# Token sums of a linear-attention layer made from one VectorE-summed tile per chunk instead of four, and the last output tile in smaller pieces

## The chip, the cores and the metric

The kernel runs on one core of a Trainium2 chip. The metric is device time in microseconds (us) of one execution, as the median of several. Engines are written as in the profile: PE is TensorE (PEld its weight loads), DVE is VectorE, ACT is ScalarE, POOL is GpSimd, SP is SyncE, which issues most transfers. L523 is line 523 of a kernel; the same instruction has a line a few numbers off in another kernel.

## The reference, cut to what matters

The input has 2048 tokens of 512 features, 32 heads of 16, and two passes of attention and feed-forward.

```python
def _A_ref(x, wqkv, wo):                   # x: 1 x 2048 x 512, H = 32, Dh = 16
    ...                                    # q, k, v from x @ wqkv
    phi = lambda t: jnp.where(t > 0, t + 1, jnp.exp(t)) + 1e-6
    pq, pk = phi(q), phi(k)
    kv = jnp.einsum("bhsd,bhse->bhde", pk, v)
    z = jnp.einsum("bhsd->bhd", pk)        # the token sum: what the change is about
    num = jnp.einsum("bhqd,bhde->bhqe", pq, kv)
    den = jnp.einsum("bhqd,bhd->bhq", pq, z)[..., None] + 1e-6
    ...                                    # (num / den) @ wo
x = x + _A_ref(_layernorm(x), A_wqkv, A_wo)
x = x + _B_ref(_layernorm(x), B_w1, B_w2)  # relu(x @ w1) @ w2, 1376 hidden
x = x + _A_ref(_layernorm(x), A_wqkv, A_wo)
x = x + _B_ref(_layernorm(x), B_w1, B_w2)
```

`z` is a sum over all tokens. Tokens lie on the 128 partitions, so somebody must add across partitions, and on this kernel that is TensorE, with a column of ones as the moving operand.

## The kernel before

The tokens are 16 tiles of 128; four tiles are a chunk. A tile of pk is 128 partitions by 512 columns of bf16. For each tile and each block of 128 columns there is one matmul with the pk block as weights and one column of ones as the moving operand; all 16 x 4 of them accumulate into four columns of one PSUM bank, from which `Zc` (the head sums) is made.

```python
def pk_unit(i):                 # the four tiles of a chunk are NCH units apart
    return (i % 4) * NCH + (i // 4)
...
def a_z_acc(lo, hi, zb, first):
    def src(i, j):
        ...                     # a GpSimd path that is switched off here
        u = pk_unit(i)
        return big[:, u * 512 + 128 * j:u * 512 + 128 * j + 128]
    def mk():
        return [(psv[:, zb, j:j + 1], src(i, j), ones[:, 0:1], first and i == lo and j == 0, i == NT - 1, True)
                for i in range(lo, hi) for j in range(4)]
    mm_group(mk, ...)           # 4 tiles x 4 blocks = 16 matmuls a chunk
```

The last output tile is finished in two halves of 256 columns, each with its last products, its own VectorE operation and its own store:

```python
prod("f3", raw(0, l1), E2, ("w2t", "b12-22"), c1, R, False)
if tail:
    rem(c1, l1, R, i1)
    out_half(i1, 1, c1)
prod("f4", summed(3), B21S, ("w2t", "b21-11"), c1, L, False)
if tail:
    rem(c1, l1, L, i1)
    out_half(i1, 0, c1)
```

All operations are recorded first and then replayed in the order of a long table, `ORDER`, found by a search; `BANKS` gives each PSUM tile its bank. An operation that two engines can do carries a letter in the table that says which does it.

## Time and profile before

| | before |
|---|---|
| time, median | 270.57 us (270.08 to 270.76, 3 runs) |
| span of the profiled execution | 268.3 us |
| PE busy | 262.3 us, 98% |
| DVE busy | 238.4 us, 89% |
| ACT busy | 199.2 us, 74% |
| one-column matmuls | 128, 25 to 26 ns from start to start |
| PE waits by name after the first 9 us | none of 0.2 us or more |

The table is read from top to bottom as one argument: PE is busy nearly always, it has no wait worth naming after the head, so PE work that goes away shortens the kernel, and anything that makes PE wait lengthens it.

### The profile page before, as it was taken

The page shows a single profiled execution, that of the slowest core. Times are in us where ns is not written, and L with a number is a line of the kernel's source. Part 1 is how long each engine was busy: PE and PEld are TensorE (multiplying, and loading weights), DVE is VectorE, ACT ScalarE, POOL GpSimd, SP SyncE. Part 2 cuts the span into 40 slices and gives each one's busy share as a digit, 9 for nine tenths or more (in the row PEclk, how much of TensorE's full clock was granted, in tenths as well). Part 3 has the DMA queues.
Part 4 walks back from the last instruction along what each step waited for, and adds up shares of the span by engine and source line. Part 5 has one row for each costly group of instructions (what it writes and reads, how often), then busy time and mean ns, then how long its engine had stood idle before and what let it go on. Part 6 is the DMA issues. An engine that isn't in the chain of part 4 may idle for free.

```text
span 268.3 us, 5363 instructions
## 1 busy us (share of the span) xinstructions
PE 262.3 (98%) x1976; PEld 172.3 (64%) x1997; DVE 238.4 (89%) x650; ACT 199.2 (74%) x434; POOL 18.7 (7%) x30
## 2 busy tenths in 40 slices
PE   7999999999999999999999999999999999999995
PEld 2444454447556878778776664455457688888884
DVE  4999986999989999998999984799889989999884
ACT  3889955999978769688867987889996878725420
POOL 4021000000110002210011000000100100200000
PEclk9999999999999999999999999999999999999999
DMA  6955882245243024402204400224363232202004
GB/s 202 381 121 82 216 286 94 101 67 119 91 123 75 0 42 86 55 0 44 56 2 78 78 5 2 98 81 85 74 157 100 41 76 45 95 2 84 16 1 156
DMA packets 47482, 23.61 MB, mean 88 GB/s; under 512 B 36736, under 2 KB 46048, under 8 KB 47456
## 3 DMA queue, kind: packets, MB, share of 16 engines
q1 hardware_dynamic: 47312, 23.21, 34.1%
q8 instruction: 15, 0.25, 0.4%
q14 instruction: 11, 0.09, 0.1%
q10 hardware_dynamic: 144, 0.07, 0.1%
HBM read 11.21 MB, written 3.15 MB: 53 GB/s over the span
## 4 chain that ended last, share of the span: by engine, by line
PE 95%; DVE 2%; DMA 1%; issue 1%; ACT 0%
PE ps L540 95%; DMA xin<-in_A_x_dram 1%; DVE bst L447 1%; DVE xn L580 0%; DVE xn L1178 0%; PE ps L503 0%; DVE mv L448 0%; DVE Tb L511 0%; DVE xn L1138 0%; ACT lnv L1169 0%; ACT rstd L1171 0%
## 5 line engine op out<-in xcount | busy, mean ns | idle before, releaser
L547 ACT ACTIVATE sqscr<-xres 128x512 bf16<-128x512 f32 x48 | 30.4, 634 | 10.8 <-DVE xres L584 5.9
L522 ACT ACTIVATE escr<-ps 128x512 bf16<-128x512 f32 x52 | 30.7, 609 | 6.8 <-PE ps L540 6.4
L520 ACT ACTIVATE big<-ps 128x512 bf16<-128x512 f32 x52 | 30.9, 613 | 1.4 <-PE ps L540 1.3
L540 PE MATMUL ps<-big,xn 128*128 128x512 bf16 x121 | 29.4, 379 | 0.4
L540 PE MATMUL ps<-gw,big 128*128 128x512 bf16 x121 | 28.9, 379 | 0.4
L1027 ACT ACTIVATE big<-ps 128x512 bf16<-128x512 f32 (+1 forms) x44 | 22.9, 533 | 6.5 <-PE ps L540 5.7
L540 PE MATMUL ps<-Tb,wqkv 128*128 128x512 bf16 x112 | 27.0, 379 | 0.0
L540 PE MATMUL ps<-wqkv,Tb 128*128 128x512 bf16 x91 | 22.7, 379 | 0.7 <-ACT Tb L510 0.3
L526 DVE TENSOR_TENSOR big<-big,escr 128x512 bf16<-128x512 bf16 x52 | 21.2, 421 | 1.5 <-ACT big L520 0.8
L540 PE MATMUL ps<-w2s,big 128*128 128x256 f16 x160 | 22.1, 272 | 0.0
L540 PEld LDWEIGHTS ps<-big,xn 128*128 128x128 bf16 x128 | 12.1, 98 | 13.9 <-issue 0.7
L540 PE MATMUL ps<-w,big 128*128 128x256 f16 (+2 forms) x113 | 20.9, 302 | 0.0
L540 PEld LDWEIGHTS ps<-gw,big 128*128 128x128 bf16 x128 | 12.2, 98 | 13.4 <-issue 0.5
L1010 ACT ACTIVATE ps<-ps 128x512 f32<-128x512 f32 (+1 forms) x29 | 15.0, 518 | 6.5 <-DVE big L1048 2.6
L540 PE MATMUL ps<-w,xin 128*128 128x256 bf16 (+1 forms) x140 | 19.5, 273 | 0.0
L540 PE MATMUL ps<-xn,xin 128*128 128x256 f16 x128 | 19.4, 273 | 0.0
L540 PE MATMUL ps<-Tb,w 128*128 128x512 bf16 x80 | 18.8, 379 | 0.0
L540 PEld LDWEIGHTS ps<-Tb,wqkv 128*128 128x128 bf16 x112 | 10.6, 98 | 12.0 <-ACT escr L522 0.3
L524 DVE TENSOR_SCALAR escr<-escr 128x512 bf16<-128x512 bf16 x52 | 14.4, 286 | 4.3 <-ACT escr L522 4.2
L540 PE MATMUL ps<-xn,w 128*128 128x256 f16 x120 | 18.2, 273 | 0.0
L540 PE MATMUL ps<-Tb,wper 128*128 128x256 bf16 x120 | 18.2, 273 | 0.0
L540 PEld LDWEIGHTS ps<-w2s,big 128*128 128x128 bf16 x160 | 15.5, 98 | 4.0 <-DVE xres L1105 0.4
(166 smaller groups left out, 548.6 us busy)
## 6 DMA issues: line engine op xcount, KB each, us to landing
xn<-rdram SPq DMA_DIRECT2D x32, 128.0 KB
wqkv<-in_A_wqkv_dram SPq DMA_DIRECT2D x3, 512.0 KB, 7.3
xin<-in_A_x_dram SPq DMA_DIRECT2D x3, 512.0 KB, 8.1
out_dram<-xn SPq DMA_DIRECT2D x3, 512.0 KB, 2.8
w<-in_B_w_dram SPq DMA_DIRECT2D x1, 1376.0 KB, 6.6
w<-in_B_w_dram SPq DMA_DIRECT2D x1, 1280.0 KB, 9.8
rdram<-rsp SPq DMA_DIRECT2D x8, 128.0 KB, 1.7
wo<-in_A_wo_dram SPq DMA_DIRECT2D x1, 512.0 KB, 10.6
```

The source lines that it names most:

```text
L447: g.add(DVE, lambda e: e.bn_stats(bst[:, i, :], xin[:, i, :]), [("xin", i)] + list(behind), [("bst", i)], C_DVE_BNST, name="bnst%d" % i)
L520: g.add(ACT, lambda e: e.activation(dst_ap, psv[:, b, :], ACTF.Identity, bias=1.0 + 1e-6, scale=1.0), [("ps", b)], [dst_key], C_ACT_PSUM, ...
L522: g.add(ACT, lambda e: e.activation(escr[:, s, :], psv[:, b, :], ACTF.Exp), [("ps", b)], [("escr", s)], C_ACT_EXP, name=name + "_exp")
L524: g.add(DVE, lambda e: e.tensor_scalar(escr[:, s, :], escr[:, s, :], 1.0, 1e-6, ALU.min, ALU.add), [("escr", s)], [("escr", s)], C_DVE_BF4 ...
L526: g.add(DVE, lambda e: e.tensor_tensor(dst_ap, dst_ap, escr[:, s, :], ALU.max), [dst_key, ("escr", s)], [dst_key], 340.0, name=name + "_phi")
L540: last = e.matmul(o, l, r, start=st, stop=sp, skip_group_check=skip)
L547: g.add(ACT, lambda e: e.activation(sqscr[:, q, :], xres[:, i, :], ACTF.Square, accum_out=dst[:, i:i + 1]), [("xres", i)], [("sqscr", q), ...
L1010: g.add_flex([(ACT, lambda e: e.activation(dst(), psv[:, src, 0:W], ACTF.Identity), cost(C_ACT_PSUM)), (DVE, lambda e: e.tensor_copy(dst() ...
L1027: g.add_flex([(ACT, lambda e: e.activation(out_ap(r, m), pv(b), ACTF.Relu), cost(C_ACT_PSUM)), (DVE, lambda e: e.tensor_scalar(out_ap(r, m ...
```

## The change

The intent is to take about two thirds of the small matmuls (84 of 128) off the engine that bounds the kernel. In seven of the eight chunks VectorE adds the four pk tiles first (two tiles plus two tiles, then the halves), into fp16, and TensorE makes the token sum of the one tile that results: 4 matmuls in place of 16. The chunk left out is the last of the first attention layer. The left half of the last output tile is cut in two quarters. `ORDER` and `BANKS` were searched anew, so instructions all over the kernel stand elsewhere.

```diff
-        def a_z_acc(lo, hi, zb, first):
-            ...
+        def a_z_acc(t, zb):
+            tiles = range(4 * t, 4 * t + 4)
+            us = [pk_unit(i) for i in tiles]
+            keys = [("big", u) for u in us] + sub_keys(us)
+            src = [unit_ap(u) for u in us]
+            if t in ZSUM[cur_layer[0] // 2]:          # ZSUM=[(0, 1, 2), (0, 1, 2, 3)]
+                zs = rhi[:].bitcast(F16)
+                hv = big[:].rearrange("p (c t k) -> p c t k", t=NCH, k=512)
+                ks = [("rhi", 0), ("rhi", 1)]
+                g.add(DVE, lambda e: e.tensor_tensor(zs, hv[:, 0:2, t, :], hv[:, 2:4, t, :], ALU.add), keys, ks, ...)
+                g.add(DVE, lambda e: e.tensor_tensor(zs[:, 0, :], zs[:, 0, :], zs[:, 1, :], ALU.add), ks, ks, ...)
+                src, keys = [zs[:, 0, :]], ks[0:1]
             def mk():
+                return [(psv[:, zb, j:j + 1], x[:, 128 * j:128 * j + 128], ones[:, 0:1], t == 0 and k == 0 and j == 0, t == NCH - 1, True)
+                        for k, x in enumerate(src) for j in range(4)]
...
-            prod("f4", summed(3), B21S, ("w2t", "b21-11"), c1, L, False)
             if tail:
-                rem(c1, l1, L, i1)
-                out_half(i1, 0, c1)
+                for q in range(2):
+                    cols = slice(128 * q, 128 * q + 128)
+                    prod("f4%d" % q, summed(3), B21S[:, :, cols], ("w2t", "b21-11"), c1, cols, False)
+                    rem(c1, l1, cols, i1)
+                    out_part(i1, cols, c1, q)
...                             # ORDER and BANKS: new tables; the unused GpSimd path is taken out
```

## The prediction

> **What bounds the kernel now.** I read the page from its top. Part 1 says TensorE (PE) is busy for 98% of the span, VectorE (DVE) for 89%; the DVE share is an average, and in many slices it too is at nine tenths. Part 4, the chain that ended last, says that 95% of the span is PE work of one line:
>
> ```profile
> span 268.3 us, 5363 instructions
> PE 262.3 (98%) x1976; PEld 172.3 (64%) x1997; DVE 238.4 (89%) x650; ACT 199.2 (74%) x434; POOL 18.7 (7%) x30
> DVE  4999986999989999998999984799889989999884
> PE 95%; DVE 2%; DMA 1%; issue 1%; ACT 0%
> ```
>
> A busy PE need not be a PE at its limit, so I looked at the waits. In the whole trace PE shows three waits by name: 1.2 us before the warm-up, then 0.3 and 0.2 us for the first copies of transposed x. The busy time in the stretch from 7.80 us (first transposes after the fill) to 265.43 us (end of the last matmul) is 256.20 of 257.63 us. Waits of a weight load of 0.2 to 0.4 us do appear; most are hidden under the running matmul. So between 7.8 and 265.4 us PE is practically never without work: the kernel ends sooner only by less PE work, an earlier start, a shorter tail after the last matmul, or it ends later by new PE stalls.
>
> The instructions that the change is about, from the groups by shape and the timeline:
>
> ```profile
> L540 PE MATMUL ps<-ones,big 128*128 128x1 bf16 x128 | 3.9, 163 | 0.0
> 18.45 0.54 PE L540 MATMUL ps<-ones,big 128*128 128x1 bf16 x16
> 18.85 1.02 PE L540 MATMUL ps<-wqkv,Tb 128*128 128x512 bf16 x4
> ...
> 37.01 1.43 PE L540 MATMUL ps<-ones,big 128*128 128x1 bf16 x48
> 38.52 0.81 PE L540 MATMUL ps<-big,xn 128*128 128x512 bf16 x3
> ```
>
> These are the token sums: 16 tiles of pk times 4 column blocks in each of two attention layers, 128 matmuls of one moving column. The reader should take the start of a group from the start of the next, because 163 ns is the latency of one, not its cost. The first 16 cost 18.85 - 18.45 = 0.40 us, 25 ns each. The four groups hold the PE for 0.40, 1.51, 1.20 and 0.41 us, together 3.52 us, or 27.5 ns each.
>
> **What the Trainium skill says.** (1) "TensorE: Matmul & The Clock Gate", section "Wait — 56ns, not 53.3ns?": the distance of matmul starts never falls below about 25 ns however few columns move. The trace agrees (25 ns in three of the four groups). So a one-column matmul costs an eighth of a 512-column one, and removing it is worth 25 ns, not nothing. (2) "VectorE: DVE Perf Modes", section "The perf-mode tier table": tensor_tensor on 16-bit SBUF data reaches the 2x mode and no higher. The trace agrees: a bf16 tensor_tensor of 512 columns lasts 417 to 421 ns, one of 1280 with fp16 output 821 ns. The slope is (821 - 417)/768 = 0.526 ns per column, two columns a cycle at 0.96 GHz. (3) "Perfetto Trace Analysis", section "Identifying the Most-Contended Engine": matmul busy time is no measure of distance from roofline. Hence the check with waits and starts above.
>
> **The change part by part.**
>
> *a. Token sums taken from PE.* Three of four chunks in the first attention layer and all four in the second are summed on DVE first. Seven chunks go from 16 matmuls to 4: 7 x 12 = 84 fewer, 44 left. At 25 to 27.5 ns this is 2.1 to 2.3 us of PE time, all on the bounding engine. I take 2.2.
>
> *b. Sums put on DVE.* Each chunk gets one tensor_tensor of 1024 columns (two tiles plus two tiles) and one of 512. Estimate for the first from the slope: 417 + 512 x 0.526 = 686 ns; the second is the 417 ns row. That is 1.10 us per chunk and 7.7 us in all by duration. Neighbouring DVE instructions start closer than their durations (36.42, 36.74, 37.09, 37.41, 37.75 us for alternating 0.29 and 0.43 us operations, a step of 0.33), so I count about 0.95 us per chunk, 6.6 us in all. The new schedule also hands work back: from the order of both kernels, DVE gets net three more 512-wide PSUM copies and one more cast, but six fewer PSUM evacuations into the hidden tiles and one transposed-copy fewer; with the rows' means the sum is about -1 us, moved to ACT, which is 74% busy. DVE then stands at 238.4 + 7.7 - 1.1 = 245 us, about 92%. It is not on the chain by its average; by stage it may be.
>
> *c. The stage where this matters.* In the first attention layer, DVE is busy 16.34 of 17 us from 16 to 33 us and 5.19 of 6 us from 33 to 39. Before the first head sum (Zc, at 38.5 us) the new order has the same 24 + 24 phi operations, three sums (2.9 us), and without the head mask pair (0.20 + 0.22 us) and one 0.42 us copy: 2.0 us more DVE work. The new PE order puts 8 more 512-column matmuls (8 x 0.216 = 1.7 us) ahead of the first matmul on Zc and loses 36 x 25 ns = 0.9 us, so Zc is wanted about 0.8 us later; roughly 0.8 us of DVE idle time was also there. 2.0 against 1.6: it about fits, with a small stall possible. I charge 0.3 us for stalls here and in the second attention layer (150 to 166 us), where DVE has more room: 13.00 busy of 16 us.
>
> *d. Last output tile.* Its left half is cut in two quarters: 6 matmuls of 256 columns become 12 of 128. The 128-column group of the trace costs 2.1/32 = 65 ns each, the 256-column ones about 110: 12 x 0.065 - 6 x 0.110 = +0.1 us of PE time. In return the last DVE operation shrinks: 256 columns take 475 ns, 512 take 745, so 128 is estimated at 340 ns, 0.13 us less. But DVE must still finish a 512-column tile (0.75 us) between the two quarters, and PE gives it only about 0.4 us (one quarter) where it gave 0.66 before:
>
> ```profile
> 264.81 0.75 DVE L580 SCALAR_TENSOR_TENSOR xn<-ps,rstdf,xres 128x512 bf16<-128x512 f32 x1 [0.28 <-PE ps L540]
> 265.05 0.10 PEld L540 LDWEIGHTS ps<-w,big 96*128 96x128 bf16 x1
> 265.16 0.27 PE L540 MATMUL ps<-w,big 96*128 96x256 bf16 x1
> 265.48 0.47 DVE L1138 SCALAR_TENSOR_TENSOR xn<-ps,rstdf,xres 128x256 bf16<-128x256 f32 x1
> 265.98 0.42 SPq L1141 DMA_DIRECT2D out_dram<-xn  x1
> ```
>
> Here PE and DVE arrive together (265.43 and 265.48). After, DVE comes later, so I expect the tail no shorter, +0.1 us; the store itself, 1.6 us from issue to landing for 64 KB, is mostly latency and hardly gets shorter with 32 KB.
>
> *e. The head.* The new order runs the statistics of tile 1 in the 0.60 us in which DVE waited for the first rstd, and sends one copy to ACT. The chain of waits goes through these DVE statistics up to 7.8 us, but PE could not take the next transposes before the first projection is issued (6.64 + 4 x 0.216 = 7.5 us, itself a little later). I expect -0.1 us.
>
> Sum: -2.2 + 0.3 + 0.1 + 0.1 - 0.1 = -1.8 us. 270.57 - 1.8 = 268.8; because a re-searched order was presumably kept for being better, I shade it to **268.6 us**, -0.7%.
>
> **The rivals.** *DVE becomes the bound.* For it: DVE is at 95% between 60 and 140 us and 96% from 16 to 33, and 6.6 us are added. Against: the 60 to 140 us stretch gets none of the sums; they lie in the two attention layers, and a third of the additional work fits in idle time. If all the first layer's excess fell on PE, some 2 us would return and the time would be about 270.5. *A new wait for the sum.* The small matmuls now wait for two dependent DVE operations. The new PE order spreads the groups of 4 between large matmuls, some microseconds after their tiles, which speaks against; at worst 0.3 us for each of seven groups, giving back 2 us. *Small matmuls were hidden anyway.* Then nothing is gained. Against: the 512-column matmuls stand 0.40 us apart around the 16. *Better than the sum.* If the head gives its full 0.5 us of statistics and no stall appears: about 267.8.
>
> **Range and chances.** The certain term is 2.1 to 2.3 us; the doubt is in the stalls (0 to 1.5 us), the tail (-0.1 to +0.4), and the head (-0.5 to 0). That makes 267.5 to 269.9. Faster than 2% would need under 265.2 us, 5.4 us less, more than twice the PE work removed; slower by 2% needs stalls of 7 us. Chances 0.02, 0.96, 0.02.
>
> **What would show it.** Right: PE keeps about 98%, 44 one-column matmuls with 1.2 us, PE busy down by about 2.1 us, DVE near 245 us, the wide sum near 690 ns and the narrow one near 420, no named PE wait over 0.3 us after 8 us. Wrong: PE idle time that names the DVE sums, Zc or a phi operation between 25 and 45 us or 150 and 170 us; a first transposed group well before 7.5 us; more than 3.2 us from the last matmul to the end (it is 268.3 - 265.16 = 3.1 now).

## The result, and the profile after

The changed kernel takes 268.98 us (median of 4 runs, 268.71 to 269.4); the kernel before, run beside it, 270.66 (270.08 to 270.93). The ratio is 0.9942, 95% interval 0.992 to 0.9964: 0.6% less, within 2%. Ratios in this text are from the fast runs of both kernels in the same rounds, so they are not quite the ratio of the medians quoted. Plain means over all listed runs give ratios within 0.0007 of them (0.9924 for tr_early and 1.0021 for sums_unread are the largest shifts).

The top of the page of the changed kernel, the answer to the first fence of the prediction (span; busy time of each engine; DVE by fortieths of the span; the chain that ended last by engine):

```profile
span 267.7 us, 5218 instructions
PE 261.2 (98%) x1901; PEld 170.0 (63%) x1919; DVE 242.4 (91%) x662; ACT 199.5 (75%) x437; POOL 18.5 (7%) x30
DVE  4999999999799999999998999599999999979884
PE 93%; DMA 3%; DVE 1%; ACT 1%; issue 1%; SPq 0%; DVEq 0%
```

Two things are to be seen. DVE took 4.0 us more work and stands at 91%. And the chain, which was PE for 95%, now has 3% of DMA in it. PE busy fell only by 1.1 us, about half of the work removed. That figure is not a good balance: 21 of 1997 matmuls have no record in the trace of before and 18 of 1919 in that of after (PE against PEld counts), and ends are modelled. The pages of halves and best, two versions told of below that have the same 1913 matmuls, all recorded, show 261.3 and 262.0 us. Starts are the better measure.

The two new VectorE operations, by tile (duration min/median/max in ns, first and last start in us, form), and the small matmuls that are left, by shape:

```profile
L615 DVE TENSOR_TENSOR rhi<-big x7: 683/684/693, 29.3 to 161.9; 128x1024 f16<-128x1024 bf16 x7
L616 DVE TENSOR_TENSOR rhi<-rhi x7: 417/418/425, 30.2 to 163.1; 128x512 f16<-128x512 f16 x7
```

```profile
L537 PE MATMUL ps<-ones,rhi 128*128 128x1 bf16 x28 | 1.7, 164 | 0.0
L537 PE MATMUL ps<-ones,big 128*128 128x1 bf16 x16 | 0.5, 163 | 0.0
```

There are 28 + 16 = 44 as counted. Their busy time of 2.2 us is again latency; the cost of a group of four is read from the starts on the timeline (start, duration, instruction):

```profile
34.38 0.24 PE L537 MATMUL ps<-ones,rhi 128*128 128x1 bf16 x4
34.48 0.81 PE L537 MATMUL ps<-wqkv,Tb 128*128 128x512 bf16 x3
```

The next large matmul starts 0.10 us after the group, 25 ns for each, where a group of 16 took 0.40 us. So the removal itself works as meant.

What had not been foreseen stands at 66 us. It is the first up-projection of the first feed-forward layer, in before and then in after (a bracket tells how long the engine sat idle and for what):

```profile
65.05 0.38 PE L540 MATMUL ps<-xn,xin 128*128 128x256 f16 x2
65.27 1.03 PE L540 MATMUL ps<-Tb,w 128*128 128x512 bf16 x4
```

```profile
65.21 0.60 PE L537 MATMUL ps<-xn,w 128*128 128x256 f16 x4
66.51 0.82 PE L537 MATMUL ps<-Tb,w 128*128 128x512 bf16 x3 [0.70 <-DMA Tb<-xn]
```

After the change PE stands idle for 0.70 us, waiting for a tile that a transfer transposes. The chain of that stretch tells where the tile came from:

```profile
...
60.89 0.61 ACT xn L555
...
61.84 4.63 DMA Tb<-xn
66.47 0.05 issue
66.51 1.69 PE ps L537 x7
```

A reader has to be careful here: the chain charges the transfer with 4.63 us, which is what "DMA 3%" mostly is, but PE was working during all but 0.70 us of them. The chain names what came last, not what was lost. The transfer is slow, too: the median of this kernel's 30 transposes from issue to landing is 3.1 us, and the slowest took 4.8.

To see where PE's savings stayed, I added up a fixed cost for each matmul by its columns (215.8 ns for 512, 109.2 for 256, 56 for 128, 42.5 for 96, 25.5 for 1, means from start to start of equal neighbours without a wait or a missing record) in the order in which PE runs them, and looked how far the actual starts run behind. By this account the PE work is 263.1 us before and 261.0 after, 2.1 less; but in the profiled executions PE lost about 1.4 us more than before: 0.40 in the head, about 0.9 between 59 and 83 us, the rest after. The profiled execution was the slowest of its kernel (269.4 us). It was not known yet whether the median execution has these losses.

The tail, answer to the last fence of the prediction:

```profile
264.28 0.75 DVE L577 SCALAR_TENSOR_TENSOR xn<-ps,rstdf,xres 128x512 bf16<-128x512 f32 x1
264.53 0.22 PE L537 MATMUL ps<-w,big 96*128 96x128 bf16 x1
264.95 0.34 DVE L1133 SCALAR_TENSOR_TENSOR xn<-ps,rstdf,xres 128x128 bf16<-128x128 f32 x1
265.32 0.37 ACTq L1137 DMA_DIRECT2D out_dram<-xn  x1
```

PE is done at 264.75 us, DVE still works on the 512-column tile, and the last quarter waits for it. From the start of the last matmul to the end of the span it is 267.668 - 264.534 = 3.13 us; before it was 268.312 - 265.156 = 3.16 (three places from the packed traces).

### The profile page after: what moved, and what is told of

It reads as the page before. It is cut to its first block, busy times and chain, and to the rows that moved or that the text cites. A ratio compares the mean times of both kernels' runs of the same rounds, so it can differ in the third digit from the quotient of the medians.

```text
span 267.7 us, 5218 instructions
## 1 busy us (share of the span) xinstructions
PE 261.2 (98%) x1901; PEld 170.0 (63%) x1919; DVE 242.4 (91%) x662; ACT 199.5 (75%) x437; POOL 18.5 (7%) x30
## 4 chain that ended last, share of the span: by engine, by line
PE 93%; DMA 3%; DVE 1%; ACT 1%; issue 1%; SPq 0%; DVEq 0%
PE ps L537 93%; DMA Tb<-xn 2%; DMA xin<-in_A_x_dram 1%; PE ps L500 0%; ACT escr L519 0%; DVE xn L577 0%; DVE bst L444 0%; ACT xn L555 0%; ACT big L517 0%; DVE Tb L508 0%; SPq L382 0%; DVE xn L1174 0%; DVEq L1398 0%
## 5 line engine op out<-in xcount | busy, mean ns | idle before, releaser
L1020 ACT ACTIVATE big<-ps 128x512 bf16<-128x512 f32 (+1 forms) x49 | 25.5, 529 | 8.6 <-PE ps L537 8.3
L537 PE MATMUL ps<-big,xn 128*128 128x512 bf16 x122 | 30.3, 379 | 0.3
L537 PE MATMUL ps<-gw,big 128*128 128x512 bf16 x121 | 29.6, 379 | 0.4
L537 PE MATMUL ps<-w,big 128*128 128x256 f16 (+3 forms) x114 | 20.9, 301 | 0.0
L537 PE MATMUL ps<-xn,xin 128*128 128x256 f16 x128 | 20.1, 273 | 0.0
L537 PE MATMUL ps<-w,xin 128*128 128x256 bf16 (+2 forms) x145 | 19.6, 269 | 0.0
L570 POOL TENSOR_TENSOR rstdf<-varf,nhalf 128x4 f32<-128x4 f32 x8 | 8.5, 1066 | 137.3 <-DVE varf L568 137.3
L1103 ACT ACTIVATE ps<-ps 128x256 f32<-128x256 f32 x26 | 9.7, 372 | 10.7 <-PE ps L537 10.1
```

The costliest lines, as they stand in the source:

```text
L537: last = e.matmul(o, l, r, start=st, stop=sp, skip_group_check=skip)
L570: g.add(POOL, lambda e: e.tensor_tensor(rstdf[:, sl], varf[:, sl], nhalf[:, 0:4], ALU.pow), [("varf", t), ("nhalf",)], [("rstdf", t)], C_P ...
L1020: g.add_flex([(ACT, lambda e: e.activation(out_ap(r, m), pv(b), ACTF.Relu), cost(C_ACT_PSUM)), (DVE, lambda e: e.tensor_scalar(out_ap(r, m ...
L1103: g.add_flex([(ACT, lambda e: e.activation(psv[:, c1, cols], psv[:, c2, L], ACTF.Identity), 290.0), (DVE, lambda e: e.tensor_copy(psv[:, c ...
```

## The experiments

My theory after the result: the 84 removed matmuls bring all of their 25 ns, the sums on VectorE cost nothing to speak of because the new order has room for them, and the quarters do nothing. The rivals: the sums cost some of it back; the head's new order costs 0.4 us; the wait at 66 us eats the first layer's share; or the new order alone is what helps, and the sums have no part in it. "Before" of a run is the kernel before on the same chip in the same rounds (11 runs each; medians 270.39, 270.05, 270.8 and 270.22 us).

| run | what it is | median us | ratio to before | 95% interval |
|---|---|---|---|---|
| (the change) | | 268.98 | 0.9942 | 0.992 to 0.9964 |
| sums_out | new order, no sums, 16 matmuls | 270.93 | 1.0015 | 0.9992 to 1.0038 |
| sums_unread | sums made but not used, 16 matmuls | 271.28 | 1.0026 | 1.0009 to 1.0044 |
| few_no_sums | no sums, 4 matmuls (wrong result) | 269.1 | 0.9947 | 0.9931 to 0.9963 |
| layer2_only | sums in the second layer only | 270.01 | 0.9973 | 0.9953 to 0.9993 |
| before_sums | old order, sums added | 275.48 | 1.0194 | 1.0172 to 1.0216 |
| before_sums_late | old order, sums placed as in the new | 273.89 | 1.0118 | 1.0099 to 1.0138 |
| halves | the change, last tile in halves | 268.86 | 0.9947 | 0.9933 to 0.9961 |
| head_back | the change, old head on VectorE | 269.08 | 0.9946 | 0.993 to 0.9961 |
| loads_later | the change, read-backs later | 269.67 | 0.9986 | 0.9962 to 1.001 |
| head_and_loads | both of the two above | 270.19 | 0.9993 | 0.9979 to 1.0007 |
| tr_early | the change, transposed tile made earlier | 268.47 | 0.9917 | 0.9896 to 0.9938 |
| best | tr_early + head_back + halves | 268.68 | 0.9944 | 0.993 to 0.9958 |

Each kernel has one execution for the profile and 4 or 5 more beside the kernel before.

### Two by two: the matmuls and the sums, each alone

**sums_out** keeps the new order and takes the sums out of it.

```diff
- ZSUM=[(0, 1, 2), (0, 1, 2, 3)]
+ ZSUM=[(), ()]                  # and the 14 entries of the sums leave ORDER
```

> The changed kernel with its own instruction order, but without the fourteen DVE sums: all 16 token-sum matmuls per chunk read the pk tiles again, at the same places. If the token sums are a plain PE cost (25 ns each) and the DVE sums are free, it is 84 x 25 ns = 2.1 us slower than the changed kernel: about 271.1 us. If the DVE sums cost PE stalls in the changed kernel, those go away here and it is less than 1.5 us slower (under 270.5). If small matmuls were hidden, no slower than 269.2.

Measured: 1.0015. The new order without the sums isn't faster than the old one; the rival "the order is what helps" falls. On the timeline of PE there is no wait at 66 us:

```profile
66.42 0.81 PE L537 MATMUL ps<-Tb,w 128*128 128x512 bf16 x3
```

The same matmul starts at 66.42 us here and at 66.51 in the changed kernel. PE arrives later, with 36 more small matmuls behind it, when the tile is there. But that is not the whole difference: the transfer itself was faster. From issue to landing the same transpose takes (changed kernel, issued at 61.84 us; then sums_out, issued at 62.83):

```profile
DMA to landing us min/median/max: 4.6/4.6/4.6
```

```profile
DMA to landing us min/median/max: 3.1/3.1/3.1
```

Had it taken 3.1 us in the changed kernel, it would have landed at 64.9 us, before PE was ready for it at about 65.65 (65.21 and four matmuls of 256 columns). By this sum the slow transfer makes the wait, and PE's earlier arrival alone would not have.

**sums_unread** makes the sums, but TensorE still reads the four tiles. The result is correct.

```diff
-                src, keys = [zs[:, 0, :]], ks[0:1]
```

> The sums are made on DVE but nobody reads them; the 16 matmuls per chunk read the pk tiles (result stays right). Against the kernel without sums it tells the DVE cost alone. If the sums fit in idle DVE time: the same time as without sums, within 0.3 us (about 271.1). If DVE has become the bound in the attention layers: 1 us or more slower than without sums.

Measured: 1.0026. Against sums_out that is 0.0011 of 270.4 us, 0.3 us for fourteen VectorE operations, and the intervals overlap widely.

**few_no_sums** has the few matmuls, but of one of the four tiles and without the sums. Its result is wrong (relative error 1.33); its work is that of the change without what the change pays.

```diff
- ZSUM=[(0, 1, 2), (0, 1, 2, 3)]
+ ZSUM=[(), ()]
+            if t in [(0, 1, 2), (0, 1, 2, 3)][cur_layer[0] // 2]:
+                src = src[0:1]
```

> Wrong on purpose: 4 matmuls per chunk read one pk tile, no sums. It has the PE work of the changed kernel and the DVE work of the old one. If the sums are free on DVE: equal to the changed kernel within 0.3 us (about 269.0). If they cost stalls: faster than the changed kernel by those stalls, 0.5 us or more (under 268.5).

Measured: 0.9947, the same as the change. The wait at 66 us is there without any sum:

```profile
66.28 1.04 PE L537 MATMUL ps<-Tb,w 128*128 128x512 bf16 x4 [0.78 <-DMA Tb<-xn]
```

What follows from the four: the 84 matmuls are worth 1.0015 - 0.9947 = 0.0068, or 1.8 us, without sums, and with sums 1.0026 - 0.9946 = 0.0080, or 2.2 us (sums_unread against head_back, which is the change but for one exchange in the head, of the same rounds). The work removed is 84 x 25.5 ns = 2.1 us. So it comes through in full, as near as this can be measured: by the intervals each of the differences is uncertain by some 0.7 us. The sums cost 0.3 us in one comparison and -0.1 in the other: not told apart from nothing. VectorE's busy time by the pages is 236.7 and 237.0 us without the sums, 242.4 and 242.6 with them: 5.4 to 5.9 us of additional work on an engine that is 90% busy, and the kernel takes no notice.

**layer2_only** leaves the sums in the second attention layer alone, to see whether the first layer's share was eaten by the wait at 66 us.

```diff
- ZSUM=[(0, 1, 2), (0, 1, 2, 3)]
+ ZSUM=[(), (0, 1, 2, 3)]
```

> The changed kernel with the DVE sums only in the second attention layer; the first one reads its pk tiles with all 64 matmuls again (36 more than the changed kernel, 0.9 us of TensorE work). Theory: the first layer's saving is mostly lost at 66 us, where TensorE then waits 0.7 us for a transposed tile; so the wait vanishes here and the time is within 0.3 us of the changed kernel (269.1). Rival: the saving of the first layer is kept: 0.9 us slower (269.9).

Measured: 0.9973, with no wait at 66 us in its trace. The first layer's 36 matmuls are thus worth 0.9973 - 0.9942 = 0.0031, or 0.8 us, against 36 x 25.5 ns = 0.9 us of work. That favours "kept" over "eaten", but the two intervals overlap; the traces below say more.

### The place of the sums

**before_sums** puts the sums into the old order, each pair right behind its chunk's last pk tile, with the old banks and the old halves; the small matmuls come two PE groups later.

```diff
  ORDER of the kernel before
+ zs, zt of each of the seven chunks, behind the chunk's last pk tile
~ the chunk's small matmuls two PE groups later
```

> The kernel before, its own instruction order and banks, with the seven sums put in by hand directly behind the last pk tile of a chunk on VectorE and the four matmuls some groups later; nothing else changed. If the saving is TensorE work and needs no new schedule: 1.5 to 2 us faster than before, about 268.8. If the sums push other VectorE work onto TensorE's path unless the whole order is searched anew: 270 or more.

Measured: 1.0194, 5.3 us slower. With as many matmuls removed as in the change, the old order loses three times what the new one gains. The page and PE's waits:

```profile
PE 264.1 (96%) x1913; PEld 169.6 (62%) x1913; DVE 245.4 (89%) x664; ACT 199.4 (72%) x434; POOL 18.9 (7%) x30
```

```profile
PE ps L537 <- DVE big L523: 3.1, 3, 1.5
PE ps L537 <- DVE ps L755: 0.9, 1, 0.9
PE ps L537 <- DVE rhi L616: 0.7, 2, 0.5
```

The columns are the total in us, the number of times, the longest. The largest wait is not for the sum (rhi) but for a pk tile (big): VectorE comes late with the ordinary work because the sums stand ahead of it. PE's worst place, and VectorE in the same microseconds:

```profile
36.69 0.25 PE L537 MATMUL ps<-ones,rhi 128*128 128x1 bf16 x4 [0.47 <-DVE rhi L616]
36.80 1.89 PE L537 MATMUL ps<-big,xn 128*128 128x512 bf16 x8
40.20 0.55 PE L537 MATMUL ps<-ones,big 128*128 128x1 bf16 x16 [1.51 <-DVE big L523]
```

```profile
35.48 0.69 DVE L615 TENSOR_TENSOR rhi<-big 128x1024 f16<-128x1024 bf16 x1
36.20 0.42 DVE L616 TENSOR_TENSOR rhi<-rhi 128x512 f16<-128x512 f16 x1
36.55 0.20 DVE L822 TENSOR_REDUCE ehead<-ident 128x8 f32<-128x32 bf16 x1
...
37.99 0.82 DVE L940 TENSOR_TENSOR wper<-w 128x1280 f16<-128x1280 bf16 x1
...
39.71 0.42 DVE L523 TENSOR_TENSOR big<-big,escr 128x512 bf16<-128x512 bf16 x1
40.05 0.82 DVE L940 TENSOR_TENSOR wper<-w 128x1280 f16<-128x1280 bf16 x1
```

VectorE has no gap here. The last pk tile is made at 39.71 and ends at 40.13, and PE starts at 40.20. Ahead of it stand the sums and work that nobody needs yet: a weight sum (wper, 0.82 us) and the head mask.

**before_sums_late** moves them: the sums go to where the new order has them, the two weight sums and the head mask behind the head sums.

```diff
  ORDER of before_sums
~ zs, zt at the places of the new order
~ two wper sums, ehead, esel: behind zc
```

> The order of the kernel before with the sums put in again, but each where the changed kernel has it: some microseconds behind its tiles, small matmuls later, and the weight sums and head mask of the first layer moved behind the first head sum. Theory: what cost 5.4 us in the first hand-made version was the place (a 1.1 us block ahead of work that others waited for), not the amount of work: well under 272, about 270. Rival: the old order has no room for 6.6 us of DVE work wherever it stands: 273 or more.

Measured: 1.0118, 273.89 us. My theory had said about 270, so it missed. Placement of the sums and of what stands beside them gives back 1.0194 - 1.0118 = 0.0076, or 2.1 us of the 5.3. The wait for the last pk tile is shorter, not gone:

```profile
38.97 0.55 PE L537 MATMUL ps<-ones,big 128*128 128x1 bf16 x16 [0.62 <-DVE big L523]
```

The run changed one thing more than the place, and this is a rival that was not tested. In before_sums all seven pairs of sums stand back to back, and 1.07 us pass from the start of the wide sum to the start of the operation behind the narrow one. In before_sums_late each pair has one other operation between its two sums, and it is 1.14 us with that operation included, which costs about 0.33 elsewhere. So a pair takes about 0.25 us less of VectorE's time when something stands in the gap, an estimate of 1.8 us for seven. Place and gap filling are not told apart. (In the changed kernel six of the seven pairs have other work between them.)

In all there are still 1.5 us of waits for pk tiles, 1.3 for the sums and 0.9 for a PSUM tile by name. What else in the new order makes the room (an order of some 1600 entries, of which hardly a stretch is the same) was not taken apart. It stays open.

### The tail and the head

**halves** is the change with the last tile in two halves as before.

```diff
-                for q in range(2):
-                    cols = slice(128 * q, 128 * q + 128)
-                    prod("f4%d" % q, ...); rem(c1, l1, cols, i1); out_part(i1, cols, c1, q)
+                rem(c1, l1, L, i1)
+                out_part(i1, L, c1, 0)
```

> The changed kernel with the last output tile in two halves again, both projections of the last pair ahead of it. My prediction charged the quarters +0.1 us of TensorE work and +0.1 us of tail: then this is 0.2 us faster (268.8). If the smaller last piece shortens the tail as intended: 0.2 us slower (269.2) or more.

Measured: 0.9947 against 0.9942. From the start of the last matmul to the end it is 266.80 - 263.64 = 3.16 us; 3.13 with quarters. The quarters do nothing in either direction.

**head_back** puts VectorE's first normalisation ahead of the second tile's statistics again, as in the kernel before. In the trace of the change these statistics waited 0.82 us for x to arrive, with the normalisation behind them.

```diff
- 8 33 29 40        # bnst1 (33) ahead of norm0 (29)
+ 8 29 33 40
```

> The changed kernel with the first normalisation put back ahead of the second statistics on DVE, as in the old order. The trace of the changed kernel has the first group of eight transposes at 8.20 us, the old one at 7.80. If that 0.40 us head loss is carried to the end: 0.4 us faster than the changed kernel, about 268.6. If it is swallowed by a later wait (the transposed tile at 66 us): the same, 269.0.

Measured: 0.9946: no gain. The traces tell why the 0.40 us of the head was no finding. The first projection on PE starts at 7.29 us in the change, but at 6.92 in few_no_sums, 6.63 in sums_out, 6.58 in sums_unread, 6.53 in halves, 6.80 in loads_later, 6.74 in layer2_only and 7.46 in tr_early, all of which have the very same head; head_back has 6.62. One trace differs from another by 0.9 us here for no reason in the kernel. What differs is when x arrives: the second transfer of x, issued at 1.24 to 1.25 us in all eight, lands between 4.35 us (halves) and 5.29 (tr_early), at 4.90 in the change, and the first projection starts 2.2 to 2.5 us after that landing.

### The wait for the transposed tile

**loads_later** tests a cause for the late tile: four read-backs of 128 KB (xn<-rdram) stand right behind it in SP's queue. They change places with the next transpose in that queue (big<-hrt), that of the remainder tile.

```diff
~ ORDER: the four read-backs of chunk 2 (396, 393, 394, 395) as one block, behind 429
```

> The changed kernel with the four read-backs of the reciprocals of chunk 2 issued after the transpose of the remainder tile, as the old order had it, instead of right behind the second transpose of chunk 0. In the changed kernel that transpose takes 4.6 us to land (3.1 for the others) and TensorE waits 0.7 us for it at 66.5 us, 1.0 at the weight load. If the read-backs are what slows the transpose: it lands in about 3.3 us, the wait is gone, 0.8 us faster than the changed kernel (about 268.2). If the transpose is late for another reason: the wait stays and the time is 269.0.

Measured: 0.9986, worse than the change, and the tile comes later, not earlier: its transfer took 5.6 us and PE stood for 1.66.

```profile
66.98 1.25 PE L538 MATMUL ps<-Tb,w 128*128 128x512 bf16 x5 [1.66 <-DMA Tb<-xn]
```

The theory fell: moving the read-backs away does not make the tile land sooner, and costs 0.0044, or 1.2 us. By itself the run doesn't clear them, since the transpose of hrt is now issued in their place, at 64.04 us, while the tile is under way. tr_early and best, below, say more: the read-backs stand as close behind the transpose there, 1.3 us, and it takes 3.2 us. **head_and_loads**, which has both edits, says the same with 0.9993 and a wait of 1.57 us.

```diff
~ ORDER: head_back and loads_later together
```

> The same and the first normalisation put back ahead of the second statistics. Alone, the latter started TensorE 0.5 us earlier but gave no time. If the wait at 66 us swallowed it, then with that wait mended both show: 1.2 us faster than the changed kernel, about 267.8. If not: as the kernel with the later read-backs alone.

**tr_early** does not touch the transfers but makes the tile that is transposed earlier: its mean (nmf) directly behind its residual on VectorE, its centring ahead of one exponential on ScalarE, and two VectorE operations that aren't urgent behind them.

```diff
~ ORDER: nmf2 (352) behind resid2; cen2 (353a) ahead of q3_3_exp (317)
~        a block sum (435d) and a weight sum (432) later
```

> The changed kernel with the four operations that lead to the late transpose put ahead on their engines (centring of tiles 1 and 2 of chunk 0 before a weight sum and an exponential). The second transpose of chunk 0 is then issued about 1 us earlier. If the 0.7 to 1.0 us wait at 66 us follows the issue: it goes, 0.7 us faster than the changed kernel (268.3). If the landing does not move with the issue, or the exponential's delay makes a new wait: 269.0.

Measured: 0.9917, the lowest, and the wait for the transfer is gone. The transpose is not issued 1 us earlier, though: counted from the group of eight projections named below, at 2.87 us in place of 3.10 (61.79 - 58.92 and 61.84 - 58.74). It takes 3.2 us to land in place of 4.6, and that is the larger part. By itself this would read as 0.7 us won, so I ran it again in **best**, together with head_back and halves.

```diff
~ ORDER: tr_early and head_back together; last tile in halves
```

> The version put together from the parts that measured best: the changed kernel with the mended place (as tr_early), the first normalisation ahead of the second statistics (as head_back) and the last output tile in halves (as halves). The mended place measured 0.3% under the changed kernel's ratio (0.9917 against 0.9942), the other two nothing to speak of (0.9946 and 0.9947). If only the mended place counts: 0.992 of the kernel before, 268.3 to 268.5 us. If the head's order counts too in the mean over runs: 0.990, about 268.0. If tr_early's gain was chance: 0.9945, about 268.9.

Measured: 0.9944, which is the change (0.9942), halves (0.9947) and head_back (0.9946) again. The third of the expectations came true. The traces tell why. PE does the same matmuls in the same order in all these kernels from a group of eight projections (ps<-Tb,wqkv) to the up-projection at 66 us (ps<-Tb,w), so the time from the one start to the other can be compared directly. First the change, then best, PE's timeline, cut to the lines that matter:

```profile
58.74 1.89 PE L537 MATMUL ps<-Tb,wqkv 128*128 128x512 bf16 x8
...
66.51 1.90 PE L537 MATMUL ps<-Tb,w 128*128 128x512 bf16 x8 [0.70 <-DMA Tb<-xn]
```

```profile
58.31 1.89 PE L538 MATMUL ps<-Tb,wqkv 128*128 128x512 bf16 x8
60.19 1.05 PE L538 MATMUL ps<-xn,w 128*128 128x256 f16 x8
...
62.38 0.84 PE L538 MATMUL ps<-w,Tb 128*128 128x96 bf16 x16
63.50 0.83 PE L538 MATMUL ps<-xn,xin 128*128 128x256 f16 x6 [0.28 <-DVE xn L970]
...
65.79 1.89 PE L538 MATMUL ps<-Tb,w 128*128 128x512 bf16 x8
```

The stretch lasts 66.51 - 58.74 = 7.77 us in the change and 65.79 - 58.31 = 7.48 in best. The wait of 0.70 us is gone, but only 0.29 us is won: a wait of 0.28 us for a sum of transposed blocks on VectorE (xn) has come in its place, and the groups ahead of it stand further apart as well. A sum made by the same line of the kernel is what sums_out waits for, where no transfer is in the way:

```profile
58.98 1.89 PE L537 MATMUL ps<-Tb,wqkv 128*128 128x512 bf16 x8
61.09 1.05 PE L537 MATMUL ps<-xn,w 128*128 128x256 f16 x8 [0.22 <-DVE xn L969]
```

| kernel | stretch, us | named waits in it, us | issue to landing of the transpose, us |
|---|---|---|---|
| sums_out | 7.44 | 0.22 for VectorE | 3.1 |
| sums_unread | 7.48 | 0.26 for VectorE | 3.2 |
| layer2_only | 7.60 | 0.38 for VectorE | 3.1 |
| tr_early, best | 7.48, 7.48 | 0.28 for VectorE | 3.2, 3.2 |
| the change, halves, head_back, few_no_sums | 7.77, 7.80, 7.80, 7.85 | 0.70 to 0.78 for the transfer | 4.6 to 4.7 |
| loads_later, head_and_loads | 8.72, 8.64 | 1.66, 1.57 for the transfer | 5.6, 5.5 |

So, as far as traces go, the wait for the transfer costs the change 0.3 us against the kernels that lack it, not the 0.70 that stand in the bracket: where the transfer is slow PE waits for it, and where it is not, PE waits 0.2 to 0.4 us for VectorE in the same stretch. These 0.3 us are 0.1% of the time, less than half of an interval's width, which is why tr_early's 0.9917 and best's 0.9944 cannot both be read as its worth. The 0.9 us that loads_later and head_and_loads add in the same stretch are most of what they lose (1.2 us for loads_later). No version beats the changed kernel by more than the spread.

What goes with the slow transfers can be read from the packets in the traces. The page counts 15 packets of a queue q8 of the kind "instruction" (0.25 MB), each of 16 KB. Of the 420 transposes of this form in the 14 traces, 70 have such a 16 KB packet that begins between their issue and their landing. All 39 that took more than 4.13 us are among these 70, and the 350 others took 4.12 at most. The packet in question begins at 63.5 to 64.5 us in the eight kernels of the table that have 36 small matmuls fewer in the first layer, so while this transpose is under way, and at 58.4 to 58.8 in sums_out, sums_unread and layer2_only, which keep them; there it meets the pair of transposes before, which took 3.9 to 4.9 us. So the removal of instructions may itself have moved the packet onto this tile. That is a reading after the fact: no run moved the packet alone, and it doesn't suffice, since tr_early and best have it too (64.28 and 63.66 us) and their transpose took 3.2 us.

## Why the prediction was right

The predicted time was 268.6 us in a range of 267.5 to 269.9; it is 268.98, and within 2% as given 96 of 100. By its own steps:

- **Step a, token sums off PE.** Right, shown by removing the step alone: 1.8 and 2.2 us measured for 2.2 predicted. The upper end of 27.5 ns was misread: between the starts at 37.01 and 38.52 there are four weight loads of the next large matmuls before the Zc group and only three matmul records, so the 1.51 us hold a large matmul (0.216 us) without a record. Without it the 128 cost 3.30 us, 25.8 ns each. The 25 ns floor is the number that carries it, and reading it from starts and not from the 163 ns column was what mattered.
- **Step b, sums on VectorE.** The durations are right to 2 ns: 684 and 418 ns for 686 and 417. The sum was too large: the sums add 5.4 to 5.9 us of busy time, where I had 6.6 by starts and 7.7 by durations, and VectorE's other work is 1.4 to 1.7 us less (238.4 before against 237.0 and 236.7), a little more than the 1.1 charged. That this went to ACT doesn't show in ACT's time, which is 199.2 us before and 199.4 to 199.7 in all versions of the new order. So VectorE stands at 242.4 us, not 245.
- **Step c, stalls of 0.3 us.** The place and the cause were wrong, and that the size comes out about right is chance. I looked for them at Zc and in the second layer, from VectorE. The one PE wait over 0.3 us after the head is 0.70 us for a transposed tile at 66 us, by DMA, of which 0.3 us are a net loss against the kernels without it. The sums do not cause it, since few_no_sums has it too; it stands where that transfer took 4.6 us or more and is absent where it took 3.1 to 3.2. It was not in the list of what could happen: the rivals spoke of engines and of the sums, and not of a transfer that becomes slower.
- **Step d, quarters.** Right in that nothing is won: the last VectorE operation lasts 0.34 us as estimated, the one before it stands in its way, and the tail is 3.13 us for 3.16 before. I expected +0.1 of tail, and +0.1 of PE work from 65 ns for each matmul of 128 columns; by the 56 and 109.2 ns from start to start it is 12 x 0.056 - 6 x 0.1092 = 0.02 us.
- **Step e, the head, -0.1 us.** Not shown. It differs by 0.9 us among executions of the same head, with the arrival of x, and head_back finds no difference in the mean.
- **The sum** was -1.8 us, giving 268.8. The result is -1.7 between medians. The 0.2 us that I then took off because a searched order was presumably kept for being better had nothing behind it, and sums_out shows that the order without the sums is, if anything, slower (1.0015). That sum and result agree to 0.1 us is partly luck, since the terms of steps c, d and e aren't each confirmed; only the 2.2 us are. The range isn't the sum of the doubts named either: with 2.3 and 2.1 us for step a these give 267.7 to 270.4, not 267.5 to 269.9.
- **The rivals.** "DVE becomes the bound" did not happen in the change, but before_sums shows that it is a true danger: with the old order the same sums end 5.3 us above the kernel before, and 6.8 us (1.0194 - 0.9942) over the change. The argument against it, that a third of the work fits in idle time and the order spreads the rest, fits the change and would have been wrong about the edit alone. "Small matmuls were hidden anyway" is refuted by the two-by-two.
- **The tests named ahead.** PE at 98%, 44 small matmuls, and both durations came true; seven groups of 0.10 us and one of 0.40 make 1.1 us for 1.2. "PE busy down by 2.1 us" failed (1.1), through the measure and not the work, and "no named PE wait over 0.3 us" failed at 66 us.

Two things stay open: what in the new order makes the room that before_sums_late still lacked, and whether the instruction packet that goes with the transposes of 4.6 to 5.6 us (median 3.1) is what slows them.

## What to carry to other kernels

When an engine bounds a kernel, even tiny instructions on it are worth their start-to-start distance, and giving them to a neighbour that is 90% busy can be free, but it needs room in the schedule: the same edit lost 1.9% and 1.2% in two placements by hand in the old order and won 0.6% in a new one. Predict the work from starts and undo single parts to measure it; do not read a wait of one trace as a gain to be had: a wait of 0.7 us was removed here, 0.3 us came of it in the trace, and nothing that could be told apart in the mean of the runs.

## What the Trainium skill lacked or had wrong

- "DMA: Bandwidth & Descriptors", section "DMA Transpose (X-bar)", lists constraints of a transposing transfer and no time to landing. The runs show 3.0 us at least, 3.1 to 3.2 in the median and 4.8 to 5.6 at most among the 30 of each kernel, and one of the slow ones stood in PE's path. What goes with the slow ones, a 16 KB instruction packet in flight with all 39 over 4.13 us, isn't in that section either.
- "Vector Engine (DVE) Microarchitecture Reference", section "Measured stream behaviour on trn2", charges about 75 ns for each instruction after queue overlap. For neighbours that do not depend on each other the trace agrees: 0.33 us from start to start for a tensor_tensor of 512 columns that lasts 0.42, where 512 columns at the 0.526 ns of the prediction and those 75 ns make an estimate of 0.34. For a pair in which the second reads the first that section has no figure: in before_sums the narrow sum starts 0.72 us after the wide one, which lasts 0.69, where in the changed kernel an operation that doesn't read it starts after 0.61.
- "TensorE: Matmul & The Clock Gate", section "Wait — 56ns, not 53.3ns?": the floor of 25 ns from start to start is given there as measured at 32 columns. The runs show it at one column and with a weight load of 128 columns for each matmul: 0.10 us for four.
- On how much two executions of the same instructions differ, I found nothing on the pages used: the first projection starts between 6.53 and 7.46 us in eight traces with the same head, after x landed between 4.35 and 5.29.
